# Weight halves, late small-row probabilities, GpSimd's pooled additions kept to one chunk, and other slots for the value folds

## The chip, the cores and the metric

One core of a Trainium2 chip runs the whole program. The metric is the device time in microseconds (us) of one execution. A profiled execution also has a span, from its first to its last instruction; the time is 1.7 to 2.2 us longer than the span (2.1 to 2.2 us in runs 3 and 13, so about 0.4 us of what they lose in time lies outside the span). Several executions of a kernel usually differ by about 1 us here, at times by more than 2, as much as the effects that this study is about, so I quote medians, spans of all executions, and ratios with a 95% interval. Where the text below calls an execution slow or quick, it means no more than a long or a short span; the granted TensorE clock was 0.997 to 1.000 throughout.

Names used below: PE is TensorE, DVE is VectorE, ACT is ScalarE, POOL is GpSimd, SP is SyncE. A "q" behind an engine's name means its instruction queue.

## The reference

Pooled attention for 8 batches, followed by a mixture of 4 experts over all 4608 tokens:

```python
k_p = k.reshape(B, H, Sp, 8, D).mean(axis=3)      # keys and values pooled by 8
v_p = v.reshape(B, H, Sp, 8, D).mean(axis=3)
attn = softmax(q @ k_p.T / sqrt(D)) @ v_p          # B=8, H=8, S=576, D=64
x = attn.transpose(0, 2, 1, 3).reshape(B * S, H * D)
p = domain_probs / (domain_probs.sum(-1, keepdims=True) + 1e-09)
for e in range(4):
    out += p[:, e:e + 1] * (relu(x @ w1[e]) @ w2[e])   # 512 -> 1024 -> 512
```

## The kernel before

Tokens are worked on in nine chunks of 512: 512 tokens of each batch, then the 8 x 64 remaining "small rows". A weight product of one expert is done as seven half-size products, each paired with one of the seven of the preceding expert's second product. Such a pair is a **slot** of about 1.87 us; an expert has 7 slots and a chunk 28, about 52 us. While chunk b-1 is multiplied, the attention of batch b is fitted into given slots by a plan. Its result goes through VectorE (`x_tok`) and is turned by a DMA transpose on SP's queue into `xT`, which the next chunk's products read.

The parts that the change and the argument touch, cut:

```python
def load_w1(e):
    n = 2 if e == 0 else 1                     # halves for expert 0 only
    ...
def load_w2(e):
    n = 2 if e in (0, 2) else 1
    ...
def load_part(b, what, part):                  # keys or values of batch b, two rows of eight at a time
    src, raw = ((k, raw_k), (v, raw_v))[what]
    nc.gpsimd.dma_start(out=raw[:], in_=rows_of(src, b, 2 * part, 2 * part + 2),
                        accum_op=ALU.add if part else ALU.bypass)
def values_folds(b): ...                       # VectorE: vp <- raw_v row 0 + row 1; frees raw_v
def turn(b, r):
    ...
    nc.sync.dma_start_transpose(out=dst, in_=x_tok)     # xT <- x_tok

def down(c, e, step, flip=0, pooled=()):       # one of seven products of the second layer
    ...
    elif step in pooled and e > 0:             # pooled = (4,): a pair of blocks goes by way of GpSimd
        for j in range(BLOCKS):
            prob = p_all[:, c * NR + row * BLOCKS + j, e:e + 1]
            nc.scalar.activation(out=addend[:, j], in_=ps[:, j], func=ACT.Copy, scale=prob)
        dst = acc[:, row * BLOCKS:(row + 1) * BLOCKS, cols]
        nc.gpsimd.tensor_add(out=dst, in0=dst, in1=addend[:])
    else:                                      # VectorE: acc += prob * ps, one instruction per block
        for j in range(BLOCKS):
            add(ps[:, j], c, e, row * BLOCKS + j, cols, first)

usual = dict(queries=-8, keys=-9, values=-2, contexts=(11, 14, 18, 21), ...,
             k=(-2, 0, 5, 9), v=(-2, 0, 5, 9), x=(22, 25, 25, 25), ...)
plans[BUSY + 1] = dict(usual, keys=-8, values=4, v=(5, 8, 12, 16))   # batch 3
```

In these traces every engine starts its instructions in the order of its program, without regard to slots: a load "of slot 26" starts as soon as GpSimd has done what stands before it and the buffer is free. And the sums of the next chunk's input (`x`, on VectorE) wait in VectorE's order for the last transpose.

The softmax here doesn't subtract the row's maximum and nothing guards it: scores larger than these inputs give would overflow.

## Time and profile before

| | before |
|---|---|
| time, median of 3 | 489.79 us (489.51 to 490.30) |
| span of the profiled execution | 488.7 us |
| busy: PE, DVE, ACT, POOL | 480.9, 378.9, 304.8, 118.4 us |
| pooled additions on GpSimd | 24, of 1267 ns |

PE is the bound. The prediction below shows the lines for that. One group that it only quotes is worth seeing whole (columns after the group: busy us, mean ns; then the idle time of the engine in front of it, and who ended most of that):

```profile
L780 POOL TENSOR_TENSOR acc<-acc,addend 128x512 f32<-128x512 f32 x24 | 30.4, 1267 | 255.1 <-ACT addend L778 213.1
```

Read it as "GpSimd stands still for 213 us because its next instruction is one of these additions".

### The profile page before, as it was taken

Reading aid. Unit: us, or ns where it says so; the run is one execution under the profiler, and the core shown is the slowest. Engines: PE = TensorE matmul, PEld = TensorE weight load, DVE = VectorE, ACT = ScalarE, POOL = GpSimd, SP = SyncE. Lnnn points to the kernel's source line nnn. Section 1 sums busy time; section 2 is a strip of 40 time slices with the busy share of each in tenths; the row PEclk is TensorE's granted clock in tenths of the full one; section 3 lists DMA queues with packets and bytes.
Section 4 is the critical chain, followed back from the end, with each engine's and each line's share of the span. In section 5 each row is a group of like instructions: output and inputs, shape, how many; then the busy total and the mean of one; then the engine's idle time right before and its main releaser. Section 6 shows DMA issues by size and latency. Waiting matters only on the chain.

```text
span 488.7 us, 11602 instructions
## 1 busy us (share of the span) xinstructions
PE 480.9 (98%) x4717; PEld 412.2 (84%) x4721; DVE 378.9 (78%) x764; ACT 304.8 (62%) x583; POOL 118.4 (24%) x118
## 2 busy tenths in 40 slices
PE   8999999999999999999999999999999999999996
PEld 4868578898888888888889889888888888888885
DVE  5789899789768976797679866997678766876674
ACT  5787445855676567656765567556755567556650
POOL 8330504242523154016411442111011101110100
PEclk9999999999999999999999999999999999999999
DMA  9999999876966679345945296311112010004003
GB/s 198 209 205 203 201 180 136 99 89 63 113 101 57 88 80 144 34 82 59 160 48 90 27 169 62 68 23 66 34 23 23 23 65 3 12 23 86 1 1 88
DMA packets 101877, 41.98 MB, mean 86 GB/s; under 512 B 73904, under 2 KB 100272, under 8 KB 101824
## 3 DMA queue, kind: packets, MB, share of 16 engines
q0 software_dynamic: 56992, 22.42, 40.4%
q1 hardware_dynamic: 43728, 17.77, 16.7%
q10 hardware_dynamic: 1104, 1.05, 0.6%
q8 instruction: 37, 0.61, 0.5%
q14 instruction: 16, 0.13, 0.1%
HBM read 45.69 MB, written 9.44 MB: 113 GB/s over the span
## 4 chain that ended last, share of the span: by engine, by line
PE 89%; DMA 8%; POOL 2%; issue 0%; DVE 0%; POOLq 0%
PE unit L698 40%; PE o_ps L766 40%; DMA w_bf<-in_moe_w_dram 8%; PE o_ps L792 3%; PE att L463 2%; PE unit L825 1%; POOL wt_bf L144 1%; PE att L388 1%; PE unit L388 1%; POOL w_bf L211 0%; PE att L517 0%; PE att L500 0%; PE unit L481 0%; POOL q_sb L181 0%; PE o_ps L825 0%
## 5 line engine op out<-in xcount | busy, mean ns | idle before, releaser
L842 DVE SCALAR_TENSOR_TENSOR acc<-o_ps,p_all,acc 128x256 f32<-128x256 f32 (+1 forms) x285 | 127.0, 486 | 50.8 <-PE o_ps L766 36.6
L766 PEld LDWEIGHTS <-H 128*128 128x128 bf16 x1320 | 129.1, 98 | 15.0
L698 PEld LDWEIGHTS <-w_bf 128*128 128x128 bf16 x1088 | 105.1, 98 | 13.1 <-DMA w_bf<-in_moe_w_dram 0.4
L678 DVE CUSTOM_DVE_ANT_0 H<-unit,partial 128x512 bf16<-128x512 f32 x128 | 87.3, 685 | 26.4 <-PE unit L698 12.2
L766 PE MATMUL o_ps<-w_bf,H 128*128 128x256 bf16 x792 | 102.6, 273 | 0.0
L698 PE MATMUL unit<-xT,w_bf 128*128 128x256 bf16 x704 | 100.5, 273 | 0.0
L780 POOL TENSOR_TENSOR acc<-acc,addend 128x512 f32<-128x512 f32 x24 | 30.4, 1267 | 255.1 <-ACT addend L778 213.1
L713 ACT COPY partial<-unit 128x512 f32<-128x512 f32 x128 | 72.3, 592 | 30.3 <-PE unit L698 30.2
L698 PEld LDWEIGHTS <-wu_bf 128*128 128x128 bf16 x816 | 77.6, 98 | 11.6 <-issue 2.5
L698 PE MATMUL unit<-xs,wu_bf 128*128 128x256 bf16 x512 | 77.0, 273 | 0.0
L766 PE MATMUL o_ps<-wt_bf,H 128*128 128x256 bf16 x528 | 68.4, 273 | 0.0
L715 ACT ACTIVATE H<-unit 128x512 bf16<-128x512 f32 x66 | 39.8, 605 | 30.9 <-PE unit L698 30.9
L766 PEld LDWEIGHTS <-S 128*128 128x128 bf16 x528 | 51.7, 98 | 6.0
L719 ACT ACTIVATE H<-unit 128x512 bf16<-128x512 f32 x66 | 39.6, 602 | 25.6 <-PE unit L698 25.3
L711 ACT COPY unit<-unit 128x512 f32<-128x512 f32 x68 | 39.4, 582 | 23.6 <-PE unit L698 18.0
L698 PE MATMUL unit<-xs,w_bf 128*128 128x256 bf16 x256 | 38.4, 273 | 0.0
L840 ACT ACTIVATE acc<-o_ps,p_all 128x256 f32<-128x256 f32 x72 | 30.7, 485 | 9.4 <-PE o_ps L766 7.9
L698 PE MATMUL unit<-xT,wu_bf 128*128 128x256 bf16 x240 | 35.7, 272 | 0.0
L154 POOL DMA_DIRECT2D kraw<-in_k_dram x20 | 26.4, 1319 | 36.7 <-DMA kraw<-in_k_dram 36.7
L766 PE MATMUL o_ps<-wt_bf,S 128*128 128x256 bf16 x264 | 34.2, 273 | 0.0
L766 PE MATMUL o_ps<-w_bf,S 128*128 128x256 bf16 x264 | 34.2, 273 | 0.0
L154 POOL DMA_DIRECT2D vraw<-in_v_dram x20 | 29.1, 1454 | 20.4 <-DMA vraw<-in_v_dram 15.2
(157 smaller groups left out, 508.4 us busy)
## 6 DMA issues: line engine op xcount, KB each, us to landing
out_dram<-acc SPq DMA_DIRECT2D x32, 256.0 KB, 4.2
w_bf<-in_moe_w_dram POOLq DMA_DIRECT2D x5, 1024.0 KB, 15.6
q_sb<-in_q_dram POOLq DMA_DIRECT2D x7, 512.0 KB, 9.9
vraw<-in_v_dram POOLq DMA_DIRECT2D x22, 144.0 KB, 6.6
kraw<-in_k_dram POOLq DMA_DIRECT2D x21, 144.0 KB, 5.5
w_bf<-in_moe_w_dram POOLq DMA_DIRECT2D x5, 512.0 KB, 18.2
wt_bf<-in_k_dram POOLq DMA_DIRECT2D x4, 144.0 KB, 5.4
wt_bf<-in_v_dram POOLq DMA_DIRECT2D x4, 144.0 KB, 4.2
```

The costliest lines, as they stand in the source:

```text
L154: nc.gpsimd.dma_start(out=raw[:], in_=rows_of(src, b, 2 * part, 2 * part + 2), accum_op=ALU.add if part else ALU.bypass)
L678: nc.vector._custom_dve(TENSOR_ADD_SAT, out=dst, in0=ps, in1=part, s0=LARGEST, s1=0.0)
L698: nc.tensor.matmul(ps[:, n * HN:(n + 1) * HN], lhsT=lhs[:, kc, f:f + P], rhs=rhs[:, kc, :], start=(not grows and n == 0 and kc == 0), stop ...
L711: nc.scalar.copy(out=banks[1][:], in_=ps)
L713: nc.scalar.copy(out=part[:, step - 2], in_=ps)
L715: nc.scalar.activation(out=quarter(0, 0), in_=ps, func=ACT.Relu)
L719: nc.scalar.activation(out=quarter(0, 1), in_=ps, func=ACT.Relu)
L766: nc.tensor.matmul(ps[:, j], lhsT=lhs[:, i, j * P:(j + 1) * P], rhs=rhs[:, i, :], start=(not grows and i == 0 and j == 0), stop=(i == HF - 1),
L780: nc.gpsimd.tensor_add(out=dst, in0=dst, in1=addend[:])
L792: nc.tensor.matmul(o_ps, lhsT=lhs, rhs=w2_bf[:, e, fc, :], start=(fc == 0), stop=(fc == FCH - 1), skip_group_check=True,)
L840: nc.scalar.activation(out=dst, in_=o_ps, func=ACT.Copy, scale=prob)
L842: nc.vector.scalar_tensor_tensor(out=dst, in0=o_ps, scalar=prob, in1=dst, op0=ALU.mult, op1=ALU.add,)
```

## The change

The intent: let the weights of experts 1 and 2 arrive in halves, so that PE can start on the first half; take two tiny loads out of the crowded start; move 42 of ScalarE's copies and 21 of GpSimd's additions to VectorE as 42 fused additions (chunk 1 keeps its three on GpSimd); and fold the pooled values of batches 4 to 7 in slots where VectorE has more room.

```diff
 def load_w1(e):
-    n = 2 if e == 0 else 1
+    n = 2 if e < 3 else 1
 def load_w2(e):
-    n = 2 if e in (0, 2) else 1
+    n = 2 if e < 3 else 1
...
-    p_all = const.tile([P, NBLK, E], F32, name="p_all")          # all 36 blocks, normalised early
+    p_all = const.tile([P, NBLK, E], F32, name="p_all")          # now 32 blocks
+    p_last = const.tile([P, NR, E], F32, name="p_last")          # small rows: loaded and normalised later
...
-        elif step in pooled and e > 0:
+        elif step in pooled and e > 0 and c == 1:
...
-            queries=-8, keys=-9, values=-2, ...
+            queries=-8, keys=-9, values=-6, ...
-        plans[BUSY + 1] = dict(usual, keys=-8, values=4, v=(5, 8, 12, 16))
+        for b in range(BUSY + 1, B, 2):                           # batches 3, 5, 7
+            plans[b] = dict(usual, values=4, v=(5, 8, 12, 16))
+        plans[BUSY + 1]["keys"] = -8
```

So batches 4 and 6 fold their values four slots earlier than before, batches 5 and 7 six slots later. With the plan of batch 5, the value loads of batch 6 move to later slots as well.

More of the change, by code (lines that the diff above doesn't have):

```diff
@@ L205, in load_w1 @@
     def load_w1(e):
-        n = 2 if e == 0 else 1
+        n = 2 if e < 3 else 1
         for i in range(n):
             fs = slice(i * F // n, (i + 1) * F // n)
-            for ks in [slice(0, HK), slice(HK, KC)] if n == 2 and i == 0 else [slice(0, KC)]:
+            for ks in [slice(0, HK), slice(HK, KC)] if e == i == 0 else [slice(0, KC)]:
                 nc.gpsimd.dma_start(
@@ L222, in load_w2, with prob_of, load_last_probs, norm @@
             )
-    NBLK = NCH * NR
+    NBLK = B * NR
     p_all = const.tile([P, NBLK, E], F32, name="p_all")
+    p_last = const.tile([P, NR, E], F32, name="p_last")
+    def prob_of(c, r, e):
+        return (p_all[:, c * NR + r] if c < B else p_last[:, r])[:, e:e + 1]
     def load_probs():
+        nc.gpsimd.dma_start(
+            out=p_all[:].rearrange("p (b r) e -> p b (r e)", r=NR),
+            in_=moe_domain_probs.rearrange("(b s) e -> s b e", s=S)[0:NT].rearrange("(p r) b e -> p b r e", r=NR),
+        )
+    def load_last_probs():
         by_batch = moe_domain_probs.rearrange("(b s) e -> s b e", s=S)
-        nc.gpsimd.dma_start(
-            out=p_all[:, 0:B * NR, :].rearrange("p (b r) e -> p b (r e)", r=NR),
-            in_=by_batch[0:NT].rearrange("(p r) b e -> p b r e", r=NR),
-        )
         for bb in range(2):
-            nc.gpsimd.dma_start(
-                out=p_all[bb * REM:(bb + 1) * REM, B * NR:NBLK, :], in_=by_batch[NT:S, bb::2, :],
-            )
-    def norm_probs():
-        tot = const.tile([P, NBLK], F32, name="tot")
-        nc.vector.reduce_sum(out=tot[:], in_=p_all[:], axis=AX.X)
+            nc.gpsimd.dma_start(out=p_last[bb * REM:(bb + 1) * REM], in_=by_batch[NT:S, bb::2, :])
+    def norm(p, nm):
+        n = p.shape[1]
+        tot = const.tile([P, n], F32, name=f"tot{nm}")
+        nc.vector.reduce_sum(out=tot[:], in_=p[:], axis=AX.X)
         nc.vector.tensor_scalar_add(out=tot[:], in0=tot[:], scalar1=1e-9)
-        inv = const.tile([P, NBLK], F32, name="inv")
+        inv = const.tile([P, n], F32, name=f"inv{nm}")
         nc.vector.reciprocal(out=inv[:], in_=tot[:])
         nc.vector.tensor_tensor(
-            out=p_all[:], in0=p_all[:],
-            in1=inv[:].unsqueeze(2).to_broadcast([P, NBLK, E]), op=ALU.mult,
+            out=p[:], in0=p[:], in1=inv[:].unsqueeze(2).to_broadcast([P, n, E]), op=ALU.mult,
         )
@@ L774, in down @@
             nc.scalar.copy(out=chains[(1 + flip) % 2][:], in_=chains[flip][:])
-        elif step in pooled and e > 0:
+        elif step in pooled and e > 0 and c == 1:
             for j in range(BLOCKS):
-                prob = p_all[:, c * NR + row * BLOCKS + j, e:e + 1]
+                prob = prob_of(c, row * BLOCKS + j, e)
                 nc.scalar.activation(out=addend[:, j], in_=ps[:, j], func=ACT.Copy, scale=prob)
@@ L835, in add @@
     def add(o_ps, c, e, r, cols, first):
-        prob = p_all[:, c * NR + r, e:e + 1]
+        prob = prob_of(c, r, e)
         dst = acc[:, r, cols]
@@ L882, in first_chunk @@
         each(*(lambda n=n: x_sum(0, n) for n in range(4)), *sums[0][0:3])
-        norm_probs()
+        norm(p_all, 0)
         up(0, 1, (0, 1))
@@ L976, in pieces_later @@
         usual = dict(
-            queries=-8, keys=-9, values=-2, scores=((2, 2), (9, 2)), contexts=(11, 14, 18, 21),
+            queries=-8, keys=-9, values=-6, scores=((2, 2), (9, 2)), contexts=(11, 14, 18, 21),
             q=1, k=(-2, 0, 5, 9), v=(-2, 0, 5, 9), x=(22, 25, 25, 25), rem=(-3, 17, 24, 25),
@@ L993, in put_each @@
                     put(start + slot, piece)
+            if b == BUSY + 1:
+                put(start + 15, lambda: norm(p_last, 1))
             if b == BUSY:
@@ L997, in pieces_later @@
                 put(start + 4, lambda: fold_wide(0, 1))
-                put(start + 5, lambda: load_q_rem(BUSY))
+                put(start + 5, lambda: load_q_rem(BUSY), load_last_probs)
                 put(start + 8, lambda: fold_wide(1, 0))
```

## The prediction

> **What bounds the kernel now.** I read the page's busy line first, then the chain of waits, then TensorE's timeline around each gap, then windows by stage, and last the other engines' timelines where the change touches them.
>
> ```profile
> PE 480.9 (98%) x4717; PEld 412.2 (84%) x4721; DVE 378.9 (78%) x764; ACT 304.8 (62%) x583; POOL 118.4 (24%) x118
> PE 89%; DMA 8%; POOL 2%; issue 0%; DVE 0%; POOLq 0%
> 25.44 25.86 DMA w_bf<-in_moe_w_dram
> ```
>
> TensorE (PE) is busy 98% of a 488.7 us span. The chain (second line) is matmuls for 89%. Its DMA part lies at the start: the third line, from the chain in order of time, is one weight transfer issued at 25.44 us and awaited until 51.30 us. In issue order it is the second weight matrix of expert 1, w2(1), loaded in one piece.
>
> ```profile
> 50.35 0.38 PE L388 MATMUL unit<-qT,kpT 64*128 64x256 bf16 x4
> 51.34 1.90 PE L792 MATMUL o_ps<-w_bf,H 128*128 128x512 bf16 x7 [0.61 <-DMA w_bf<-in_moe_w_dram]
> ```
>
> Here is what the chain means: the matmuls from 50.35 us end at 50.73 us, then PE idles 0.61 us for that matrix. Busy time does not say whether matmuls run at their peak, so I checked the cadence: from 68 us on, groups of eight 256-column matmuls start 0.87 us apart, 109 ns each. By stage:
>
> ```profile
> 52.00:66.00 14.00, 13.95 (x108) 7.31 (x108) 13.16 (x26) 4.29 (x8) 6.24 (x8) 1.00 1.29 198
> 66.00:84.00 18.00, 17.95 (x184) 15.01 (x183) 17.46 (x36) 10.67 (x20) 5.81 (x6) 1.00 1.17 151
> 84.00:130.00 46.00, 46.00 (x450) 39.91 (x449) 38.95 (x81) 31.25 (x59) 15.49 (x13) 1.00 0.78 86
> 130.00:300.00 170.00, 170.00 (x1670) 149.77 (x1669) 130.29 (x264) 111.82 (x216) 55.48 (x46) 1.00 0.71 88
> ```
>
> The columns after the length are busy us of PE, PEld, DVE (VectorE), ACT (ScalarE) and POOL (GpSimd), then granted clock, DMA share and GB/s. After 52 us PE has about 0.1 us of idle time in 432 us, at clock 1.00. So between 52 us and the last matmul at 484.3 us nothing can be won by feeding PE better; the change removes no matmul. What is left: the 0.61 us, about 2 us of warm-up and waits in the first 16 us, and the tail after 484.3 us.
>
> **What the Trainium skill says.** (1) "TensorE: Matmul & The Clock Gate", section Back-to-back issue gap, gives N/2.4 + 2.5 ns for a warm isolated matmul: 109 ns for 256 columns. The trace agrees (0.87/8), so PE is at its floor. (2) "GPSIMD Engine Reference", section 3.1, has GpSimd's two-input add 1.96 times slower than VectorE's, and section 4.1 says GpSimd has no PSUM port. Both fit: a pooled addition first takes two ScalarE copies out of PSUM, and then GpSimd's add of 128x512 takes 1267 ns. (3) "DMA: Bandwidth & Descriptors", Specifications, asks for at least 512 B per transfer for line rate. Half rows of w1 are 2 KB read and 1 KB written; w1(0) moves so already, and the queue carried 203 GB/s at 10 to 20 us against 205 at 20 to 30 us. I count no cost for halving.
>
> **The change part by part.**
>
> Weights by halves. DMA is saturated until after 52 us (DMA share above 1.1, about 205 GB/s in 16-bit bytes written), and weights land in order of issue. w2(1) is 1024 KB. Its first half lands 524 KB / 205 GB/s = 2.6 us before the whole, at about 51.3 - 2.6 = 48.7 us; PE asks for it at 50.73 us. The first output block uses the first half for 4 matmuls of 512 columns, 4 x 216 = 0.86 us, and reaches the second half at 50.8 + 0.9 = 51.7 us, after it has landed at 51.3. So the 0.61 us wait goes, less an issue gap: **-0.55 us** on the path. The halves of w1(1) and w1(2) come where PE shows next to no wait (9.95 and 10.00 us busy in each 10 us from 20 to 50 us): 0. Three more DMA issues cost GpSimd 3 x 0.77 = 2.3 us. That hides, because GpSimd is already held back there:
>
> ```profile
> 13.00 0.84 POOL L211 DMA_DIRECT2D w_bf<-in_moe_w_dram  x1
> 14.17 0.76 POOL L220 DMA_DIRECT2D w_bf<-in_moe_w_dram  x1 [0.33 <-DMA w_bf<-in_moe_w_dram]
> 15.50 0.74 POOL L220 DMA_DIRECT2D w_bf<-in_moe_w_dram  x1 [0.57 <-DMA w_bf<-in_moe_w_dram]
> 18.04 0.74 POOL L211 DMA_DIRECT2D w_bf<-in_moe_w_dram  x1 [1.79 <-DMA w_bf<-in_moe_w_dram]
> ```
>
> Counting issues, the 17th, 18th and 19th each start as the 9th, 10th and 11th land: at most 8 seem to be under way at once. With halves those 8 hold fewer bytes, still over 10 us of traffic by my count, so the DMA engines do not starve.
>
> Small rows' probabilities late. Two loads of 4 KB leave the queue ahead of w1(2). GB/s dips at 24 to 27 us to 195, 178 and 191, some 0.25 us of traffic for all three probability loads; the two are perhaps 0.1 us of it. VectorE's wait for probabilities (1.37 us at 23.8) shrinks a little; PE does not wait behind it. The late normalisation is four small VectorE instructions, under 1.2 us by the sizes at 23.8 to 25.3 us, at about 148 us where VectorE is 78% busy. On the path: 0.
>
> Pooled adds. The trace has 24, each a 128x512 add. They belong to step 4 of (chunk 0, expert 3), of experts 1 to 3 in chunks 1 to 7, and of 1 and 2 in chunk 8: 1 + 21 + 2 = 24. Chunk 1 keeps 3, so 21 move. GpSimd loses 21 x 1.27 = 27 us, ScalarE 42 x 0.47 = 20 us, VectorE gains 42 scalar-tensor-tensor of 0.478 us = 20 us (a pair takes 0.79 us start to start). Its load from 130 to 484 us goes from 76% to about 81%. No engine becomes the bound by that sum; what counts is whether the queue in front of VectorE ever grows past PE's slack. Its densest later stretch:
>
> ```profile
> 324.37 0.68 DVE L678 CUSTOM_DVE_ANT_0 H<-unit,partial 128x512 bf16<-128x512 f32 x1
> 324.97 0.42 DVE L338 TENSOR_TENSOR vp<-vraw 72x512 bf16<-72x512 bf16 x1
> 325.30 0.68 DVE L678 CUSTOM_DVE_ANT_0 H<-unit,partial 128x512 bf16<-128x512 f32 x1
> 326.00 0.88 DVE L842 SCALAR_TENSOR_TENSOR acc<-o_ps,p_all,acc 128x256 f32<-128x256 f32 x2
> ...
> 331.31 0.88 DVE L842 SCALAR_TENSOR_TENSOR acc<-o_ps,p_all,acc 128x256 f32<-128x256 f32 x2 [1.25 <-PE o_ps L766]
> ```
>
> The moved pair goes in just before the second line, and the change takes that values fold (0.33 us start to start) out of this slot. Net lateness 0.79 - 0.33 = 0.46 us; the 1.25 us idle ahead of 331.31 absorbs it within 6 us. At slots with the key sums (like 311.5 us) the lateness is 0.79 - 0.18 idle = about 0.6 us. The tightest consumer is the copy of one bank into another, which needs the H sum of VectorE before it: that copy must end about 1.15 us after PE's step 0 and takes 0.57 us. I work out 0.4 us of slack left at 313 us. So no PE stall, but not by much. Sum for this part: **0**, with a tail of up to 0.1 us at each of 20 places.
>
> Values folds. They move between slots; 0.42 us each, no more work. For batch 4 the fold moves 4 slots earlier, to about 162.5 us; its last load was issued at 155.33 us, and at a typical 5.7 us it lands at 161. On the path: 0, with little margin.
>
> Sum: 489.79 - 0.55 + 0 = about **489.2 us**.
>
> **Rivals.**
> (a) VectorE becomes late and PE stalls: for it, 20 us more work in an in-order queue, and a stretch from 53.28 to 83.11 us already without an idle gap, into which one moved pair falls at 77 us. Against it, in that stretch additions still start within 0.4 us of their matmuls, and gaps of 1.38 and 1.49 us follow by 90 us. If 20 moved pairs each cost PE 0.1 us, the gain is eaten by 2 us: 490.7 to 491.2.
> (b) The wait for w2(1) is only moved: the second half, the two VectorE weight sums behind it or the next matrix may be awaited. By bytes, w2(2) lands at about 59.4 us and PE needs its second half at 60.6, so it stays clear by 0.6 us after the shift. If it returned: 489.8.
> (c) GpSimd, no longer standing behind additions (213 us of waits for the scaled copies), issues key and value loads earlier and they collide with PE-side transposes. DMA peaks of 1.2 at 130 to 140 and 180 to 190 us exist already without a PE gap, and earlier issue spreads them: 0.
> (d) More gain than that would need PE idle time, which is not there. Even with all 2 us of the start it would be 487.5.
>
> **Range and chances.** The before kernel's runs spread 489.51 to 490.30, so the gain is about the size of its noise. Best case 0.9 us of gain and a low draw: 488.4. Worst case in the range, rival (a) at about a third of its size with the gain: 490.3. A 2% change is 9.8 us: faster is impossible without removing matmuls, 0.005; slower would need half a microsecond at each of 20 places, 0.015; within, 0.98.
>
> **What would show it.** Right: the TensorE gap at 51 us gone and everything after it some 0.55 us earlier; VectorE at about 399 us busy, ScalarE about 285, GpSimd about 94; only 3 pooled adds; matmul groups of eight still 0.87 us apart from 70 to 480 us. Wrong: PE gaps of 0.1 us or more released by VectorE or by a ScalarE copy near the moved adds or the values folds; a new wait for a weight half between 20 and 66 us; a VectorE wait for value rows at about 162 us. The prediction fails most likely through many small stalls of the kind of rival (a).

## The result, and the profile after

| | before | after |
|---|---|---|
| time, median of 6 runs each | 489.92 us (489.51 to 490.46) | 491.09 us (490.03 to 492.09) |
| ratio after / before | | 1.0023 (1.0007 to 1.0039) |
| spans of after's six runs | | 490.4, 488.9, 489.7, 489.0, 489.8, 488.3 us |
| busy: PE, DVE, ACT, POOL of the profiled run | 480.9, 378.9, 304.8, 118.4 | 481.8, 393.7, 287.5, 94.3 |

Ratios are the mean time of one kernel's fast runs over that of the other's of the same rounds, so not quite the ratio of the medians. The kernel is within 2%, as predicted, but slower, and its median lies outside the predicted range. It also spreads more: 2.1 us between its shortest and longest span. The profile shown is that of the slowest of the six.

The busy line and the chain's shares by engine, after:

```profile
PE 481.8 (98%) x4717; PEld 412.3 (84%) x4721; DVE 393.7 (80%) x810; ACT 287.5 (59%) x541; POOL 94.3 (19%) x100
PE 84%; DMA 6%; DVE 5%; issue 1%; POOL 1%; ACT 1%; POOLq 0%; ACTq 0%
```

The work moved as planned. But the share of VectorE in the chain rose from 0% to 5%. PE's timeline at 51 us shows what was won (start, duration, then in brackets the idle time before, if any):

```profile
50.36 0.38 PE L392 MATMUL unit<-qT,kpT 64*128 64x256 bf16 x4
50.68 1.90 PE L796 MATMUL o_ps<-w_bf,H 128*128 128x512 bf16 x7
```

The wait of 0.61 us for w2 of expert 1 is gone. The windows by stage, with the columns as in the prediction, say where something was lost:

```profile
84.00:130.00 46.00, 45.83 (x447) 39.52 (x446) 38.98 (x81) 30.58 (x58) 15.29 (x13) 1.00 0.83 86
130.00:300.00 170.00, 168.98 (x1655) 148.28 (x1653) 135.35 (x284) 103.92 (x197) 44.18 (x37) 1.00 0.77 89
```

Before, PE was busy for all of both stretches. Now it lacks 0.17 us and 1.02 us. Busy time is a rough guide to a loss, since the ends of matmuls are modelled; so I also took the ScalarE copy that each product group starts with as a milestone and subtracted its start times in the two traces. The kernel after leads by 0.67 us at 66 us, by 0.33 at 93 us and 0.27 at 161 us. At 171 us it is **1.72 us behind**, from 188 to 343 us by 1.37 to 1.38 us, and from 357 us to the end by 1.66 to 1.67 us. Most of what was lost was lost at one place, around 170 us (1.6 us that stay lost); another 0.3 us go at 357 us (see after run 16). The first place is the border between two chunks. PE's timeline there, after:

```profile
169.90 0.60 PE L702 MATMUL unit<-xT,w_bf 128*128 128x256 bf16 x4
171.11 0.60 PE L702 MATMUL unit<-xs,w_bf 128*128 128x256 bf16 x4 [0.61 <-DVE H L682]
171.90 1.03 PE L770 MATMUL o_ps<-wt_bf,H 128*128 128x256 bf16 x8 [0.19 <-DVE acc L846]
173.15 1.03 PE L702 MATMUL unit<-xT,w_bf 128*128 128x256 bf16 x8 [0.22 <-ACT unit L715]
```

The brackets blame VectorE, which looks like rival (a) of the prediction. VectorE's own timeline shows that it is not overloaded: it stands idle for 1.89 us in front of the sum that reads `xT`. "Issue" means that the profile cannot name what ended the wait. After, then before:

```profile
166.61 0.87 DVE L846 SCALAR_TENSOR_TENSOR acc<-o_ps,p_all,acc 128x256 f32<-128x256 f32 x2
169.37 0.42 DVE L254 TENSOR_TENSOR xs<-xs,xT 128x512 bf16<-128x512 bf16 x1 [1.89 <-issue]
```

```profile
166.95 0.88 DVE L842 SCALAR_TENSOR_TENSOR acc<-o_ps,p_all,acc 128x256 f32<-128x256 f32 x2 [0.34 <-PE o_ps L766]
167.74 0.41 DVE L250 TENSOR_TENSOR xs<-xs,xT 128x512 bf16<-128x512 bf16 x1
```

The chain of waits, in order of time, leads to the last transpose of batch 3's activations, issued at 163.10 us. It counts the transpose until VectorE goes idle, and calls the rest "issue".

```profile
163.10 4.39 DMA xT<-x_tok
167.49 1.87 issue
169.37 0.42 DVE xs L254
```

The view of that tile gives 6.2 us from its issue to its landing: 163.10 + 6.2 = 169.3, the start of the sum. That the transpose ended the wait is inferred from this; in run 3 below the profile itself names it on PE. Before, the transpose was issued at almost the same time, 163.07, and landed after 3.8 us. What else was on the DMA queues? GpSimd's timeline from 157 us, before:

```profile
157.12 1.26 POOL L780 TENSOR_TENSOR acc<-acc,addend 128x512 f32<-128x512 f32 x1 [0.41 <-ACT addend L778]
169.66 1.27 POOL L780 TENSOR_TENSOR acc<-acc,addend 128x512 f32<-128x512 f32 x1 [11.28 <-ACT addend L778]
170.88 0.87 POOL L154 DMA_DIRECT2D kraw<-in_k_dram  x1
```

and after:

```profile
157.92 0.83 POOL L154 DMA_DIRECT2D kraw<-in_k_dram  x1 [1.28 <-DVE kp L297]
163.39 0.82 POOL L154 DMA_DIRECT2D vraw<-in_v_dram  x1 [4.64 <-DVE vp L342]
165.85 1.40 POOL L154 DMA_DIRECT2D kraw<-in_k_dram  x1 [1.64 <-DMA kraw<-in_k_dram]
```

Before, GpSimd stood 11.28 us in front of a pooled addition, and the first loads of batch 5 came after it, at 170.9 us. After, nothing holds them: the first goes at 157.9 us, the second at 163.4, as soon as the fold of batch 4's values (now four slots earlier, at 162.67) has freed its buffer. They run beside the transpose. In the DMA view from 158 to 170 us GpSimd's queue moved 0.15 MB before (20.1% of the 16 engines' time) and 0.52 MB after (83.0%).

A smaller loss sits at 88.7 us, on ScalarE:

```profile
88.71 0.84 ACT L844 ACTIVATE acc<-o_ps,p_all 128x256 f32<-128x256 f32 x2 [0.53 <-DMA out_dram<-acc]
```

The store of chunk 0's last block, issued at 80.07 us, took 8.55 us to land, and ScalarE may not overwrite `acc` before. GpSimd's loads of 80.06 to 81.80 us (before) had moved to 77.57 to 79.31 us (after). Before, the store issued at 80.0 us landed after 3.7 us; in run 2 below, which holds GpSimd at its old places, after 2.8 us, and there is no such wait.

### The profile page after: what moved, and what is told of

Same layout as the page of the kernel before. It is cut to its first block, busy times and chain, and to the rows that moved or that the text cites. A ratio compares the mean times of both kernels' runs of the same rounds, so it can differ in the third digit from the quotient of the medians.

```text
span 490.4 us, 11535 instructions
## 1 busy us (share of the span) xinstructions
PE 481.8 (98%) x4717; PEld 412.3 (84%) x4721; DVE 393.7 (80%) x810; ACT 287.5 (59%) x541; POOL 94.3 (19%) x100
## 4 chain that ended last, share of the span: by engine, by line
PE 84%; DMA 6%; DVE 5%; issue 1%; POOL 1%; ACT 1%; POOLq 0%; ACTq 0%
PE unit L702 39%; PE o_ps L770 38%; DMA w_bf<-in_moe_w_dram 3%; DVE acc L846 2%; DMA out_dram<-acc 2%; PE unit L829 1%; PE att L467 1%; DMA wt_bf<-in_v_dram 1%; PE o_ps L621 1%; DMA xT<-x_tok 1%; POOL wt_bf L144 1%; DVE H L682 1%; PE att L392 1%; PE unit L621 1%; PE unit L638 1%
## 5 line engine op out<-in xcount | busy, mean ns | idle before, releaser
L846 DVE SCALAR_TENSOR_TENSOR acc<-o_ps,p_all,acc 128x256 f32<-128x256 f32 (+1 forms) x298 | 132.3, 484 | 34.0 <-PE o_ps L770 22.4
L715 ACT COPY unit<-unit 128x512 f32<-128x512 f32 x68 | 39.3, 581 | 27.9 <-PE unit L702 16.6
L154 POOL DMA_DIRECT2D kraw<-in_k_dram x20 | 27.9, 1397 | 81.4 <-DMA kraw<-in_k_dram 42.0
L154 POOL DMA_DIRECT2D vraw<-in_v_dram x20 | 26.1, 1305 | 55.6 <-DMA vraw<-in_v_dram 36.4
L844 ACT ACTIVATE acc<-o_ps,p_all 128x256 f32<-128x256 f32 x64 | 27.3, 485 | 8.6 <-PE o_ps L770 6.5
```

The costliest lines, as they stand in the source:

```text
L715: nc.scalar.copy(out=banks[1][:], in_=ps)
L844: nc.scalar.activation(out=dst, in_=o_ps, func=ACT.Copy, scale=prob)
L846: nc.vector.scalar_tensor_tensor(out=dst, in0=o_ps, scalar=prob, in1=dst, op0=ALU.mult, op1=ALU.add,)
```

## The experiments

**Theory A**: the freed GpSimd lets loads go earlier, onto the DMA engines beside the transposes; a transpose lands late, VectorE waits in order, PE with it. **Rival V**: VectorE itself is too busy with its 42 additional instructions. **Rival S**: something at the start (halves, late probabilities) is at fault. Every run came with executions of the kernel before on the same chip. First four kernels and a control.

**1. Only the start.** Everything of the change but the pooled additions and the values' slots, which are as before.

```diff
-        elif step in pooled and e > 0 and c == 1:
+        elif step in pooled and e > 0:
-            values=-6, ...                                  # usual
+            values=-2, ...
-        for b in range(BUSY + 1, B, 2): plans[b] = dict(usual, values=4, v=(5, 8, 12, 16))
-        plans[BUSY + 1]["keys"] = -8
+        plans[BUSY + 1] = dict(usual, keys=-8, values=4, v=(5, 8, 12, 16))
```

> The changed kernel with GpSimd's adds in all chunks and the values folds in their old slots again: only the weight halves and the late probabilities remain. Both theories (A: loads run ahead once GpSimd is free; B: VectorE is overloaded by the moved adds) expect the gain of the first stage to stay: about 489.3 us, 0.6 us below the kernel before, no TensorE gap at 51 us nor at 170 us. If it is 490 or more, the start's parts lose time themselves.

Measured: 490.01 us, ratio 0.9998 (0.9984 to 1.0012). Mean span 488.17 us against 488.43 of the kernel before in the same rounds. No gap at 51 us, none at 170 us. Rival S falls as the cause of a loss. A gain of the start does not show either: 0.26 us is within the noise of these spans, and the interval of the ratio takes in 0.8 us of gain and 0.6 us of loss. What the halves win is read from traces after run 16.

**2. All moved additions, but GpSimd held at its old places.** After each moved pair GpSimd copies one column of the block that VectorE has just added to. It costs 0.2 us of GpSimd and makes it wait as it used to; VectorE has all its new work.

```diff
+            if step in pooled and e > 0 and c != 1:
+                nc.gpsimd.tensor_copy(out=pace[:], in_=acc[:, row * BLOCKS + 1, cols.start:cols.start + 1])
```

> The changed kernel, with one GpSimd copy of 128x1 after each moved pair of adds, which reads what VectorE has just added: GpSimd stands still at the same places as before, but does not add. VectorE keeps the 42 moved adds. A (loads run ahead of the activation transposes in the DMA queues): the 2 us stall near 170 us and the 0.34 us near 89 us go, 489.3 us. B (VectorE overload): still about 491.

Measured: 490.07 us, 0.9997 (0.9984 to 1.0010); five spans from 487.8 to 488.8. The page's busy line:

```profile
PE 481.4 (99%) x4721; PEld 412.4 (84%) x4721; DVE 393.8 (81%) x810; ACT 287.7 (59%) x541; POOL 98.6 (20%) x121
```

VectorE is as busy as in the kernel after (393.8 against 393.7 us) and nothing is lost at 170 us (0.3 us is at 357 us, see after run 16). Rival V falls as the cause of the loss at 170 us. The last transpose landed after 2.4 us.

**3. The moved additions left out altogether.** VectorE is unloaded and GpSimd free. The result is wrong (relative error 0.58).

```diff
-        elif step in pooled and e > 0 and c == 1:
+        elif step in pooled and e > 0:                            # ScalarE's copies in every chunk
...
-            nc.gpsimd.tensor_add(out=dst, in0=dst, in1=addend[:])
+            if c == 1:
+                nc.gpsimd.tensor_add(out=dst, in0=dst, in1=addend[:])
```

> Wrong result on purpose: the moved adds are dropped altogether (ScalarE still scales them out of PSUM), so VectorE has 20 us less work than in the changed kernel while GpSimd stays as free. A: stalls remain, 490.3 to 491.5 us, with a VectorE wait on the transposed activations near 167 us. B: no stall, about 489.3.

Measured: 491.58 us, 1.0026 (1.0007 to 1.0045), spans 488.0 to 490.6. VectorE did only 378.7 us of work, yet the profiled execution has the largest gap of all, and here PE's own wait names the transpose (PE, then VectorE):

```profile
170.43 0.61 PE L702 MATMUL unit<-xT,w_bf 128*128 128x256 bf16 x4 [0.94 <-DMA xT<-x_tok]
172.22 0.60 PE L702 MATMUL unit<-xs,w_bf 128*128 128x256 bf16 x4 [1.18 <-DVE H L682]
```

```profile
170.47 0.43 DVE L254 TENSOR_TENSOR xs<-xs,xT 128x512 bf16<-128x512 bf16 x1 [3.55 <-issue]
```

The transpose landed after 7.2 us. Together, runs 2 and 3 turn the two suspects around: much VectorE work with GpSimd held costs nothing at 170 us; little VectorE work with GpSimd free costs up to 2.6 us. Run 3 keeps all of ScalarE's copies too, so ScalarE's lighter load is not needed for the loss.

**4. After, but the values folded in their old slots.**

```diff
-            values=-6, ...                                  # usual
+            values=-2, ...
-        for b in range(BUSY + 1, B, 2): plans[b] = dict(usual, values=4, v=(5, 8, 12, 16))
-        plans[BUSY + 1]["keys"] = -8
+        plans[BUSY + 1] = dict(usual, keys=-8, values=4, v=(5, 8, 12, 16))
```

> The changed kernel with the values folds in the slots of before. A: the values loads of batch 5 wait for the later fold (slot 26 rather than 22), so less of them lies in front of the transposes near 165 us: the stall there shrinks or goes, 489.5 to 490.5. B: the moved pair and the values fold share slot 26 again, so it gets no better: 491 or more.

Measured: 490.27 us, 1.0000 (0.9988 to 1.0013), five spans from 488.2 to 488.8. The first key load still went early, at 157.63 us, but the value load only at 170.22 us. So with the spans as they are it takes both parts of the change, a free GpSimd and the earlier fold. The profile alone would not show this: its last transpose was issued early, at 161.57 us.

**5. Control: the kernel after again.**

> The changed kernel itself once more, as a control beside the next three on the same chip: 490.5 to 491.5 us, with runs spread over 2 us, and in a slow run a TensorE gap near 170 us.

Measured: 490.57 us, 1.0009 (0.9994 to 1.0025); spans 488.0 to 490.0. The profiled execution was a quicker one (489.0 us): PE stood still for 0.33 us at 89.7 us, behind ScalarE's wait for the store, but nothing at 170 us, with its loads as early as in the first profile. So the loss comes and goes, and one profile is not proof of how often. Of all 13 spans of this kernel (first six, these six, look 12) 5 are 489.3 us or longer; of the 42 of the kernel before that were taken beside the experiments it is 3, of up to 490.1 us, and none of these was profiled. The table after run 13 shows what differs.

**6. After, with the sums asking later.** If only VectorE's order makes the late landing costly, moving the sums should help.

```diff
-            x=(22, 25, 25, 25), ...
+            x=(22, 26, 27, 27), ...
```

> The changed kernel with the last three sums of the next chunk's activations one to two slots later (26, 27, 27 in place of 25, 25, 25), so that VectorE asks for the transposed activations 1.8 to 3.5 us later. A (VectorE, in order, stands still on late transposes): the gap near 170 us goes and the time falls to about 489.5 to 490. B (VectorE overloaded): 491 still, as the amount of its work is the same.

Measured: 491.46 us, 1.0027 (1.0009 to 1.0044). A miss. In the profiled execution, a quick one of 488.6 us, it did work: the transpose landed 5.6 us after 162.56, at 168.2 us, and the sum at 168.69 had no wait. The timed executions reached 490.5 us all the same. The first product of the next chunk reads `xT` itself (run 3 shows PE waiting for it at 170.43), so a late enough landing hurts whatever VectorE does. That this happened in the slow executions of run 6 was not seen; it stays open.

**7. GpSimd held once per chunk, at slot 26.**

```diff
+            if step in pooled and e > 0 and c > 1 and e == 2:
+                nc.gpsimd.tensor_copy(out=pace[:], in_=acc[:, row * BLOCKS + 1, cols.start:cols.start + 1])
```

> The changed kernel with GpSimd's 128x1 copy only at slot 26 (step 4 of expert 2, chunks 2 and on), which is in program order just ahead of the first loads for the next batch. A: enough to remove the gap near 170 us, 489.6 to 490.2. If the loads let go at the other places matter as much, it stays above 490.5.

Measured: 490.46 us, 1.0012 (0.9996 to 1.0027); four spans from 488.2 to 488.8, but two at 489.6 and 490.2. It helps in part. Looks 10 and 11 pursue the two slow ones.

**8. The kernel before, with loads of its own at about the early times.** Three loads of data that it does not need: keys, half as many values, keys. VectorE and the rest are as before.

```diff
+                after_add(20, HD, lambda: load_part(BUSY + 1, 0, 0))
+                after_add(23, 0, lambda: spare_v(slice(0, 4)))
+                put(start + 23, lambda: load_part(BUSY + 1, 0, 1))
```

> The kernel before with its GpSimd adds, and with three loads added that it does not need: keys at slot 20 and values and keys at slot 23 of batch 3, at 158 to 165 us, as the changed kernel issues them. VectorE's work is the same as before. A: TensorE gap near 170 us of 1 to 2.5 us, in some runs at least; 490.5 to 492.5. B: no gap, 490.1 like the kernel before.

Measured: 490.51 us, 1.0005 (0.9992 to 1.0017), no gap. A miss. The value load was half size and came at 164.25 us, 0.9 us later than in the kernel after; and in this execution the last transpose was issued early, at 160.99 us, so that its 5.7 us still ended in time, at 166.7. In look 16 at the same kernel it was issued at 163.01 us, before the value load of 164.63, and landed after 4.3 us. So the test had not reproduced the condition of the theory. Run 13 does so.

**9. After, with only batch 4's fold put back.**

```diff
+        plans[BUSY + 2] = dict(usual, values=-2)
```

> The changed kernel with one fold moved back: batch 4's values at slot 26 of batch 3's plan, as before, not at 22; all else changed. Theory A2: this fold frees the values buffer at 163 us, the loads of batch 5 start then and lie in the DMA queues ahead of the transposes of batch 4's activations, and the fold itself is only about 1 to 4 us behind its last load; both go with this one move. A2 expects 489.8 to 490.3 us and no run with a span over 489.0. If VectorE's moved adds, or the other folds, cost time, runs at 489.5 and over stay.

(One slip: the transposes at 163 us are of batch 3's activations, not batch 4's.) Measured: 490.14 us, 1.0004 (0.9990 to 1.0017); spans 488.0 to 488.8, and one of 489.3, the profiled one. There the key load at 157.99 us was still early, the transpose landed after 4.8 us, and VectorE waited 0.36 us; another 0.58 us was lost at 89 us to the store. So batch 4's fold alone is most of it, not quite all.

**10 and 11. Two looks at run 7's kernel, 12 one at the kernel after.** No edit, to catch slow executions.

> A further look at the kernel with GpSimd's stop at slot 26 only, whose runs were spread from 488.2 to 490.2: a profile of a slow run is wanted. If it is slow, A2 expects VectorE to stand still at batch 4's values fold near 162 us, as its last load comes late. A fast one has a span of 488.2 to 488.8 and no gap.

> The same kernel once more, for the same reason: slow with VectorE waiting for the last values load near 162 us, or fast without a gap there.

> A further look at the changed kernel itself: a span of 488 to 490.5, and where it is over 489.3 a TensorE gap near 170 us, released by VectorE or by the transposed activations.

Look 10 was slow (491.52 us), and not where I expected it: not a VectorE wait for values at 162 us (the fold had none), but at the chunk border before, at 117 us:

```profile
117.26 0.42 DVE L255 TENSOR_TENSOR xs<-xs,xT 128x512 bf16<-128x512 bf16 x1 [1.15 <-DMA xT<-x_tok]
```

Here the profile names the transpose. But VectorE waits for it at this border in every profile, by 0.21 us in the kernel before, 0.56 in look 15, 0.95 in look 16 and 1.02 in run 2, and in none of the other profiles is a PE gap named there. What only look 10 has is that the third sum meets a pooled addition of GpSimd (in this chunk GpSimd still does its three) and takes 1.49 us in place of 0.42 (VectorE, then GpSimd):

```profile
117.93 1.49 DVE L255 TENSOR_TENSOR xs<-xT,xs 128x512 bf16<-128x512 bf16 x1
```

```profile
117.82 1.32 POOL L785 TENSOR_TENSOR acc<-acc,addend 128x512 f32<-128x512 f32 x1 [9.41 <-ACT addend L783]
```

By the milestones this border cost 1.45 us, of which 1.07 are the longer sum. The change is not shown to be behind it. Look 11 was fast (490.10 us, no gap). Look 12, of the kernel after, gave 491.43 us with the loss at 170 us again, VectorE waiting 1.34 us for a transpose that landed after 5.7 us; no loss at 89 us in that run. So the loss at 170 us is not an accident of the first profile.

**13. The kernel before with early loads, done right.** As run 8, with the keys at 158.11 us, the full amount of values at 162.88 and keys at 166.11. They are triggered by an earlier sum on VectorE.

```diff
+                put(start + 20, lambda: load_part(BUSY + 1, 0, 0))
+                put(start + 23, lambda: nc.gpsimd.tensor_copy(out=pace[:], in_=state[("xs", BUSY + 2 - 1)][:, 0, 0, 0:1]),
+                    spare_v, lambda: load_part(BUSY + 1, 0, 1))
```

> The kernel before with the same three kinds of load as in e8, now let go as early as the changed kernel does: keys at about 157.8 us, values right after the first sum of the next activations (about 163 us, not 164.3) and in full size, keys again at about 165 us. VectorE's work as before. Theory A2 (loads in the DMA queues ahead of the last activation transposes): the transposes issued at 163.1 us land at 5 us or more after issue, in some runs a TensorE gap near 170 us and spans of 489 to 490.5. If spans stay at 487.6 to 488.9, early loads alone don't make the loss, and the moved VectorE work must take part.

Measured: 492.55 us, **1.0040** (1.0023 to 1.0058); five of six spans from 490.0 to 490.7 against a mean of 488.3 before. VectorE's work is that of the kernel before. Its timeline, and then PE's:

```profile
169.35 0.43 DVE L251 TENSOR_TENSOR xs<-xs,xT 128x512 bf16<-128x512 bf16 x1 [1.75 <-issue]
169.69 1.49 DVE L251 TENSOR_TENSOR xT<-xT 128x512 bf16<-128x512 bf16 x1
```

```profile
172.17 0.60 PE L699 MATMUL unit<-xs,w_bf 128*128 128x256 bf16 x4 [1.63 <-DVE H L679]
```

The transpose landed after 6.0 us, the wait is 1.75 us: early loads alone are enough. This shows the cause in the other direction. One reservation on its size: the second sum took 1.49 us in place of 0.42, because it ran beside GpSimd's pooled addition of 169.44 to 170.91 us, which the kernel after does not have there. By the milestones this execution goes from 0.23 us ahead at 161 us to 1.99 behind at 188 us. Of these 2.2 us the longer sum is 1.07, so the late landing alone accounts for about 1.2 (an estimate from this one profile). In span the six executions lose 1.6 us on average.

The table puts the profiles side by side: when the last transpose was issued, how long it took, what GpSimd's queue moved from 158 to 170 us, and VectorE's wait in front of the sum.

| profile | issued, us | to landing, us | GpSimd's queue, MB | VectorE's wait, us |
|---|---|---|---|---|
| before | 163.07 | 3.8 | 0.15 | 0 |
| 11, held at slot 26 | 163.07 | 3.6 | 0.13 | 0 |
| 2, held everywhere | 161.66 | 2.4 | 0.03 | 0 |
| 4, old slots | 161.57 | 4.6 | 0.15 | 0 |
| 16, before with run 8's loads | 163.01 | 4.3 | 0.49 | 0 |
| 9, batch 4's fold back | 163.04 | 4.8 | 0.29 | 0.36 |
| 5, after (quick run) | 162.07 | 4.6 | 0.45 | 0 |
| 12, after | 162.90 | 5.7 | 0.55 | 1.34 |
| after | 163.10 | 6.2 | 0.52 | 1.89 |
| 13, before with early loads | 163.25 | 6.0 | 0.51 | 1.75 |
| 3, additions left out | 163.22 | 7.2 | 0.53 | 3.55 |

VectorE reaches the sum at 167.0 to 167.7 us if nothing holds it. From 163.1 us that leaves about 4.3 us for the transpose. The seven profiles that are left out (1, 6, 7, 8, 10, 14 and 15) have no wait there. The amount in the fourth column alone does not decide: look 16 has nearly as much and a landing of 4.3 us; its value load starts 1.6 us after the transpose, that of the kernel after 0.3 us after it. But run 8, with a half-size value load 3.3 us after its early transpose, had 5.7 us, so when exactly a load slows the transpose is not settled. The transpose has to be issued late **and** to be slowed for a loss. The second is the change's doing. The first varies from run to run in either kernel, and SP's timeline shows with what: the transpose of the queries just before it holds SP's queue for 2.67 to 2.98 us in runs 2, 4 and 5, but for 4.31 us in the kernel before, 5.11 in run 11, 4.71 in run 12 and 4.80 in the kernel after. The 18 profiles show with what this goes: where GpSimd's last value load of batch 4 starts by 153.9 us (runs 2, 4, 5, 7, 8, 10, 14), the queries' transpose holds the queue for 1.9 to 3.1 us; where it starts at 154.3 us or later (all others, the kernel before too), for 4.3 to 5.5 us. So it may be a load beside a transpose once more; no run moves that load alone, so this is not shown. The late issue explains why the loss comes and goes: the kernel before has the late issue as well and gets away with it, since its transpose lands in 3.8 us.

**14. A mend: attention's last two contexts two and one slots earlier,** so that the last transpose is issued earlier.

```diff
-            contexts=(11, 14, 18, 21), ...
+            contexts=(11, 14, 16, 20), ...
```

> The changed kernel with the last two attention products of each batch at slots 16 and 20 in place of 18 and 21, so that the last transpose goes out about 1.8 us earlier, all else changed. A2: the stall near 170 us goes, spans of 487.8 to 488.9, about 489.9 us. If VectorE's load were the cause, this would be no better: 490.5 to 491.5.

Measured: 491.06 us, 1.0024 (1.0012 to 1.0036). The mechanism answered: the transpose went at 159.27 us, landed after 4.2 us in spite of 0.6 MB beside it, and the gap at 170 us is gone. The time did not: the lead over the kernel before now falls by about 0.27 us once per chunk (0.68, 0.41, 0.13, -0.15 us at 82, 158, 210, 262 us). At each place ScalarE's copy from one bank to the other waits for VectorE:

```profile
160.52 0.57 ACT L715 COPY unit<-unit 128x512 f32<-128x512 f32 x1 [0.20 <-DVE H L682]
```

VectorE was 9.73 us busy from 150 to 160 us, against 9.06 in the kernel after and 8.61 in the one before. Here, with contexts put into an already full slot, rival V's worry is real: VectorE's slack there is thin with the moved additions.

**15. One more look at the kernel before, and 16 at run 8's kernel,** for the wait at 51 us.

> The kernel before once more, for a second profile of the wait at 51 us: the prediction took 0.61 us from one profile as a constant. If the first profile was typical, 0.5 to 0.7 us again. If that wait comes and goes with the DMA queues, 0 to 0.3 us.

> The kernel of e8 once more (up to 158 us it is the kernel before): a further sample of the wait at 51 us. In e8 it was not there; constant would be 0.5 to 0.7 us, coming and going 0 to 0.7.

Measured: 489.93 and 490.46 us. The wait for w2 of expert 1 is 0.36 us in look 15. No wait is named at that place in looks 8, 13 and 16, all with the start of the kernel before. The group starts at 51.34, 50.83, 50.62, 51.09 and 50.89 us in the five profiles with that start, on average 50.95. In the 13 profiles with the halves it starts between 50.48 and 50.89 us, on average 50.67, and none has a wait there: about 0.3 us won.

**What the moved additions do cost.** At 357 us PE loses 0.3 us behind a copy of ScalarE, in all 11 profiles in which VectorE does the moved additions (the copy starts 0.50 to 0.51 us after ScalarE went idle), and in none of the other 7 (0.22 us each; runs 1, 3, 8, 13, looks 15 and 16 and the kernel before). Before, then after:

```profile
355.82 0.57 ACT L774 COPY o_ps<-o_ps 128x512 f32<-128x512 f32 x1 [0.22 <-PE o_ps L766]
```

```profile
357.49 0.57 ACT L778 COPY o_ps<-o_ps 128x512 f32<-128x512 f32 x1 [0.51 <-PE o_ps L770]
```

So the moved additions go with a steady loss as large as what the halves win. The same 11 profiles have 42 fewer instructions on ScalarE, and the chain of run 2 calls the time in front of the copy "issue" (0.33 us), not a wait for VectorE; so a full VectorE is not shown to be the reason, and which of the two it is was not tested.

No kernel beats the one before: the best three, runs 1, 2 and 4, are within 0.03% of it.

## Why the prediction was right or wrong

**The wait at 51 us.** Right in kind: the halves remove it and no weight half is awaited in its place between 20 and 66 us on PE. The term of 0.55 us was mis-sized. It was read from a single profile, where the wait was 0.61 us; it was 0.36 us in another and not seen in three more. The halves win about 0.3 us in the traces; in the times of run 1 this does not come out of the noise.

**Small rows' probabilities.** Right: the late loads at 74 us and the late normalisation (four instructions, 0.78 us in all in run 14's trace) show no wait on PE.

**Pooled additions.** The busy times of VectorE, ScalarE and GpSimd were predicted as 399, 285 and 94 us, and measured as 393.7, 287.5 and 94.3; 42 more fused additions are there. VectorE's 20 us were too many because the sum took the additions at their full length of 0.478 us, while they overlap: a pair starts 0.79 us after the one before it, as the prediction says itself, and 21 x 0.79 is 16.6 us. Run 2 shows that they cause no stall at 170 us. The sum of 0 was still not quite right: 0.3 us at 357 us goes with them. ("Both fit", on the two engines' additions, is too strong: no addition of the same shape on VectorE is in the traces. The nearest, a pair of fused ones, starts every 0.79 us against 1267 ns on GpSimd, 1.6 times as long.)

**The values folds.** The step "On the path: 0, with little margin" looked at what the fold waits for, and there it was right: the fold at 162.67 us waited for no load. It did not look at what the fold lets go. Freeing the buffer four slots earlier let the next value load start at 163.39 us.

**The step that failed is rival (c)**: "DMA peaks of 1.2 at 130 to 140 and 180 to 190 us exist already without a PE gap, and earlier issue spreads them: 0." I had the right mechanism in hand and set it to zero with an average. A peak without a gap only shows that nothing urgent was under way in that stretch. The question was which transfers the early loads would meet. From 160 to 170 us the DMA share was only 0.61 before; it rose to 1.57 after, so earlier issue did not spread the load but made a new peak just there. The loads meet the last transpose of a chunk, with about 4.3 us to spare between its issue and VectorE's need; it went from 3.8 to 6.2 us. The cost is 0 to 2.6 us, depending on the run. The gain of 0.3 us is used up by the 0.3 us at 357 us, and there is a second, smaller cost that looks to be of the same kind (0.3 to 0.6 us, in some runs, where ScalarE waits at 89 us for a store; it has no experiment of its own, runs 1 and 2 only show that it is absent with GpSimd held). So the median rose by 1.2 us.

**Rival (a)**, to which I gave the wide side of the range, predicted 490.7 to 491.2. The time measured, 491.09, falls into it, for another reason: had I only looked at the time, or only at PE's brackets ("<-DVE"), I would have called it confirmed. Runs 2, 3 and 13 refute it as the cause of the loss at 170 us.

**The class** (within 2%) was right. The range was too narrow on the slow side.

What stays open: the slow executions of run 6 were not seen in a profile; the loss at the border at 117 us (look 10) was seen once, and whether the kernel before has it too in some executions is not known, nor what its own three long spans are; the delay at 357 us is tied to the moved additions but not explained; and what moves the value load before the query transpose, and with it the time of the last transpose, was not tested.

## What to carry to other kernels

An in-order engine that waits also paces everything behind it in its program, loads above all; before you take its waits away, list what it will issue earlier and which urgent transfer will be on the same DMA engines then. Read a wait back to its first cause: PE was held by VectorE, VectorE by a transpose, the transpose by loads that nobody was waiting for. When an effect is as large as the spread between runs, look at several profiles of each kernel before you put a size on a wait.

## What the Trainium skill lacked or had wrong

- "DMA: Bandwidth & Descriptors", section Queues, rings and completion order, says that each DMA engine takes turns between queues, packet by packet; what was seen does not contradict it, but no figure is given for what that costs a transpose. Here one of 128 x 512 16-bit elements (128 KB) took 2.4 us while GpSimd's queue moved 0.03 MB from 158 to 170 us, and 3.8, 6.2 and 7.2 us with 0.15, 0.52 and 0.53 MB; but also 4.3 us with 0.49 MB (look 16) and 5.7 us with 0.37 MB (run 8). The same page's fit for one of GpSimd's DMAs (section Anatomy of one DMA, 2.0 us plus bytes over 436 GB/s) gives, as an estimate, about 2.3 us for a key or value load of 144 KB; the page of the kernel before shows medians of 5.5 and 6.6 us. These loads run beside others and most of them add to what is there, so this does not show the fit to be wrong for a load by itself.
- "TensorE: Matmul & The Clock Gate", section Back-to-back issue gap, gives about 131 ns per 512-column matmul in a stream with weight loads and calls N/2.4 + 2.5 ns the isolated case that overcounts. The trace differs: eight such matmuls take 1.73 us in a stream, 216 ns each, which is the "isolated" value (and which the same page gives elsewhere for back-to-back matmuls).
- "SBUF — State Buffer", section Who interferes with whom, says that a VectorE instruction with two SBUF inputs and a GpSimd instruction that reads SBUF exclude each other. Run 13 and look 10 agree and give a size: 1.49 us for a sum of 0.42 us that met a pooled addition of 1.47 and of 1.32 us.
- No page has it that taking waits off GpSimd moves its loads forward into other transfers: the first load moved from 170.9 to 157.9 us here.
